# Linear attention and an MLP on one core: loads moved to ACT's queue, the reciprocal moved behind two decode steps, the drain reordered

## The chip, the cores and the metric

The kernel runs on one core of one Trainium2 chip. The metric is the device time of one execution in microseconds: 1163.93 us as the median of 3 runs before the change (1163.46 to 1164.61). Five engines work side by side, each through its own instructions in order: PE (matrix products; PEld is its weight load), DVE (vector), ACT (activations), POOL (GpSimd) and SP (which here only issues transfers). An engine that comes to an instruction whose input is not there stops until it is. A transfer (DMA) is issued by an engine into that engine's queue and then moved by 16 DMA engines that all queues share.

## What is computed

```python
def _attn_ref(q, k, v, w_phi):                     # q, k, v: 8 batches x 8 heads x 576 x 64
    def phi(x):
        proj = np.einsum('bhsd,df->bhsf', x, w_phi)                  # w_phi: 64 x 128
        proj = proj - np.max(np.abs(proj), axis=-1, keepdims=True)
        return np.concatenate([np.exp(proj), np.exp(-proj)], axis=-1)
    q_p, k_p = (phi(q), phi(k))
    kv = np.einsum('bhsf,bhsd->bhfd', k_p, v)
    z = np.sum(k_p, axis=2)
    num = np.einsum('bhsf,bhfd->bhsd', q_p, kv)
    den = np.einsum('bhsf,bhf->bhs', q_p, z)[..., None] + 1e-06
    return (num / den).astype(np.float32)

def _moe_ref(x, w_in, w_out):                      # x: 4608 x 512, d_ff = 2048
    h = x @ w_in
    g = h - np.tanh(h)
    return (g @ w_out).astype(np.float32)
```

The attention output, with heads side by side, is the input x of the MLP. The MLP's weights come as float64 and are brought to float32 on the chip.

## The kernel before

**Attention.** The 64 batch-head pairs are worked off as 32 units of two heads. Unit i needs `qk` (both projections' inputs, 576 KB, `load`, L192) and `v` (320 KB, `load_v`, L198). A software pipeline works on five units at once: `period(i)` (L454) names them `a` = unit i, `c` = i-1, `p` = i-2, `r` = i-3 and `q` = i-4. `ramp` starts the pipeline with units 0 to 2, periods 3 to 31 follow, `drain` empties it. Everything from `ramp` to `drain` stands in one block in which every engine executes in the order of the code, so a line moved in `period` moves on its engine and nowhere else.

In a period, on PE: `project(a)` into the PSUM banks `pj`, `pa` and `pt`; the denominators of `r` (`pu`, L341); the sums of `p`'s keys (L299); the turning of `p`'s kv matrix (L316) and of `c`'s projections (`ptt`, L247); `kv(c)` (`pc`, L278); the numerators of `p` (`po`, L327). On DVE: `centre` (the absolute maximum `m`, L235, and the subtraction, L236, which gives `t`) for the three parts; the copy of `kv`; then the reciprocal of the denominators, L365; then three functions of the weight decode. On ACT: the copy `dd` of the denominators (L355), `kst` (L305), the decode's first step (`dec_0`, L171), the exponentials of queries and keys, and the copy `d` of the numerators (L351). On POOL: `kadd` (four sums of the exponentials of `c`'s keys, L288 to L291), then the multiplication of numerators by reciprocals (`den_mul`, L379).

**The path of a quotient.** PE leaves the denominators of `r` in four PSUM rows. `denom_copy` brings them to `dd`, a transfer spreads them over 128 partitions (`dn`, L360), DVE takes the reciprocal (`rn`, L365), a transfer stores it in DRAM (`rr`, L370); in the next period two transfers read it back, repeated over 64 partitions each (`rb`, L375), POOL multiplies, and the product is stored in `xs` (L382), from where the MLP reads x (`xl`, L112). There is one `dd` buffer, and two of `d`, so the copy `d` of unit p waits for the multiplication of unit q.

**The weight decode.** One 128 x 512 tile of `w_in` or `w_out` (512 KB as float64, `raw`, two buffers) is decoded in each period: `dec_0` on ACT into the second half of the bank `pt`, after `centre` has read the first; `dec_1` (two instructions, L175 and L176), `dec_2` (L179) and `dec_3` (L183, into the tile `wi` or `wo`) on DVE. The next period's `project(a)` writes the same bank `pt`, so its last part waits for `dec_3`. In periods 4 to 17 ACT and POOL also split one decoded tile into a high and a low part (L90, L96).

**Transfers.** All of them are issued by SP in the order of the code, but for the projection weights `wph`, which ACT issues at the start. SP too executes in order: an issue that waits holds up those behind it.

**The MLP.** x is worked off in nine groups of 512 tokens, each through 16 tiles of the 2048 hidden units: 12 matmuls into `ph` (L599), the activation on ACT and DVE, the split into `gh` and `gl` (L627, L628), 12 matmuls into `po` (L642 to L645). Each x tile is split into high and low parts by `x_split` (ACT's cast, L117; DVE's subtraction, L118). The first group's four tiles are loaded in period 30 and split in the drain.

## Time and profile before

| | |
|---|---|
| median of 3 runs | 1163.93 us (1163.46 to 1164.61) |
| profiled execution: its time / its span | 1164.22 us / 1162.3 us |
| PE, PEld busy | 1109.3 us (95%), 866.5 us (75%) |
| DVE, ACT, POOL busy | 837.1 us (72%), 771.1 us (66%), 439.2 us (38%) |
| steady attention periods (first `pj` of period 4 to that of 31) | 39.85 to 344.20 us |
| MLP with PE busy throughout | from about 388 us to the end |
| mean granted PE clock | 0.994 |

A row of the timeline reads: start, duration, engine, line, operation, output<-input with shapes, and in brackets how long the engine stood idle before it and which instruction ended that wait. "SPq" and "ACTq" are the issues of transfers by SP and ACT. In the chain of waits a DMA's row runs from its issue to its landing. A row of the groups by line gives the busy time, the mean of one instruction in ns, and the idle time ahead of the group with its releasers. A matmul's end is modelled, so the start of the next one is the better mark. Line numbers are those of the kernel before.

### The profile page before, as it was taken

To read this page: it belongs to the slowest core of one execution; us is meant where nothing else is said; L and a number is where in the kernel's file an instruction comes from. 1 tells how busy PE (TensorE), PEld (TensorE's weight loads), DVE (VectorE), ACT (ScalarE), POOL (GpSimd) and SP (SyncE) were. 2 spreads that over 40 slices of the span, in tenths; PEclk is the share of its full clock that TensorE was granted. 3 is DMA by queue.
4 is the path that set the end of the run, shared out by engine and by line. 5 is a ranking of instruction groups with operands and counts; after the bars stand their busy time and mean duration, and the time that the engine had idled before them with its cause. 6 is when DMAs were issued, how large, how long until landed. Compare 5 with 4: busy or idle time off the path is not lost.

```text
span 1162.3 us, 18558 instructions
## 1 busy us (share of the span) xinstructions
PE 1109.3 (95%) x6956; PEld 866.5 (75%) x6956; DVE 837.1 (72%) x1166; ACT 771.1 (66%) x1394; POOL 439.2 (38%) x349
## 2 busy tenths in 40 slices
PE   7989898888989999999999999999999999999997
PEld 5656565555665788888888888888888888888886
DVE  5777778777787976766766766766766766776664
ACT  4767676666666776666666666666666666666664
POOL 4676767555554554232222222222222222222222
PEclk9999999999999999999999999999999999999999
DMA  5456566565655001101001001001001001000000
GB/s 185 137 169 201 167 188 185 179 187 168 195 160 164 16 1 37 48 31 37 37 1 37 37 1 37 37 1 37 36 1 39 34 1 41 33 1 7 31 1 37
DMA packets 51018, 85.45 MB, mean 74 GB/s; under 512 B 13296, under 2 KB 24688, under 8 KB 50928
## 3 DMA queue, kind: packets, MB, share of 16 engines
q1 hardware_dynamic: 50768, 84.20, 23.4%
q8 instruction: 55, 0.90, 0.3%
q14 instruction: 35, 0.29, 0.1%
q10 hardware_dynamic: 160, 0.07, 0.0%
HBM read 65.08 MB, written 19.02 MB: 72 GB/s over the span
## 4 chain that ended last, share of the span: by engine, by line
PE 72%; DMA 14%; DVE 10%; ACT 2%; issue 1%; SPq 1%; POOL 0%; POOLq 0%; ACTq 0%; DVEq 0%
PE ph L599 33%; DMA dn<-dd 12%; PE po L642 11%; PE po L645 11%; PE po L643 11%; PE pu L341 2%; DVE pt L179 2%; DVE pt L176 2%; DVE t L236 1%; DVE m L235 1%; DVE pt L175 1%; PE pt L219 1%; DVE wi L183 1%; DVE wo L183 1%; PE pc L316 1%
## 5 line engine op out<-in xcount | busy, mean ns | idle before, releaser
L628 POOL TENSOR_TENSOR gl<-s,gh 128x512 fp32r<-128x512 f32 x144 | 185.9, 1292 | 556.2 <-ACT gh L627 547.7
L606 ACT ACTIVATE y<-ph 128x512 f32<-128x512 f32 x144 | 86.2, 599 | 252.2 <-PE ph L599 252.2
L615 DVE SCALAR_TENSOR_TENSOR s<-s,y 128x512 f32<-128x512 f32 x144 | 102.3, 710 | 186.5 <-ACT s L608 185.4
L599 PE MATMUL ph<-xh,whi 128*128 128x512 f32 x576 | 224.3, 389 | 0.4 <-DVE s L621 0.4
L642 PE MATMUL po<-who,gh 128*128 128x512 f32 x572 | 222.8, 389 | 1.8 <-ACT gh L627 1.8
L599 PE MATMUL ph<-xl,whi 128*128 128x512 f32 x576 | 224.1, 389 | 0.0
L599 PE MATMUL ph<-xh,wli 128*128 128x512 f32 x576 | 224.1, 389 | 0.0
L643 PE MATMUL po<-wlo,gh 128*128 128x512 f32 x572 | 222.6, 389 | 0.0
L645 PE MATMUL po<-who,gl 128*128 128x512 f32 x572 | 152.9, 389 | 0.0
L621 DVE COPY_PREDICATED s<-mk,th 128x512 f32<-128x512 uint32 x128 | 122.5, 957 | 13.4 <-DVE th L620 0.5
L642 PEld LDWEIGHTS po<-who,gh 128*128 128x128 f32 x572 | 107.4, 188 | 25.0 <-ACT gh L627 2.7
L599 PEld LDWEIGHTS ph<-xh,whi 128*128 128x128 f32 x576 | 108.0, 187 | 23.6 <-DVE s L621 0.8
L599 PEld LDWEIGHTS ph<-xl,whi 128*128 128x128 f32 x576 | 108.2, 188 | 22.5
L599 PEld LDWEIGHTS ph<-xh,wli 128*128 128x128 f32 x576 | 108.1, 188 | 22.4
L645 PEld LDWEIGHTS po<-who,gl 128*128 128x128 f32 x572 | 107.4, 188 | 22.4
L643 PEld LDWEIGHTS po<-wlo,gh 128*128 128x128 f32 x572 | 107.3, 188 | 22.2
L608 ACT ACTIVATE s<-y,bias_t 128x512 f32<-128x512 f32 x144 | 104.4, 725 | 0.5 <-POOL gl L628 0.5
L614 ACT ACTIVATE mk<-y,bias_t 128x512 f32<-128x512 f32 x144 | 103.4, 718 | 1.4 <-DVE s L621 1.4
L618 DVE SCALAR_TENSOR_TENSOR s<-s,ph 128x512 f32<-128x512 f32 x144 | 98.8, 686 | 5.2
L617 DVE SCALAR_TENSOR_TENSOR s<-s,s 128x512 f32<-128x512 f32 x128 | 89.0, 695 | 16.2 <-ACT s L610 3.5
L272 ACT ACTIVATE kp<-t 128x1024 f32<-128x1024 f32 (+1 forms) x128 | 90.5, 731 | 11.7 <-DVE t L236 10.5
L610 ACT ACTIVATE s<-y,bias_t 128x512 f32<-128x512 f32 x128 | 92.2, 720 | 0.9 <-POOL gl L628 0.9
(98 smaller groups left out, 1701.9 us busy)
## 6 DMA issues: line engine op xcount, KB each, us to landing
qk<-in_qkT SPq DMA_DIRECT2D x31, 576.0 KB, 4.2
v<-in_v SPq DMA_DIRECT2D x32, 320.0 KB, 5.3
rb<-rr SPq DMA_DIRECT2D x64, 144.0 KB, 4.8
xs<-rb SPq DMA_DIRECT2D x32, 288.0 KB, 2.2
out<-o SPq DMA_DIRECT2D x36, 256.0 KB, 2.0
rawi<-in_moe_w_in SPq DMA_DIRECT2D x16, 512.0 KB, 4.2
rawo<-in_moe_w_out SPq DMA_DIRECT2D x16, 512.0 KB, 4.6
xl<-xs SPq DMA_DIRECT2D x24, 256.0 KB, 4.2
```

What stands on the lines that cost most here:

```text
L272: nc.scalar.activation(u.kp[h, :, j, s, :], u.t[r][h, :, x, :], AF.Exp, scale=1.0 - 2.0 * s)
L599: nc.tensor.matmul(h, wt[:, c * P : (c + 1) * P], x[:, c, 0:N], start=(i == 0), stop=(i == 3 * NCT - 1))
L608: nc.scalar.activation(s1, y, AF.Square, bias=bias_t[:, 0:1])
L610: nc.scalar.activation(s2, y, AF.Square, bias=bias_t[:, 1:2])
L614: nc.scalar.activation(mk, y, AF.Relu, bias=bias_t[:, 2:3])
L615: nc.vector.scalar_tensor_tensor(s1, s1, PC1, y, ALU.add, ALU.mult)
L618: nc.vector.scalar_tensor_tensor(gs, gs, PA, h, ALU.mult, ALU.mult)
L621: nc.vector.copy_predicated(gs, mk.bitcast(U32), hh)
L628: pin(nc.gpsimd.tensor_tensor(gl, gs, f32(gh), ALU.subtract))
L642: nc.tensor.matmul(po[t], a, wo[f][0], start=(f == 0), stop=False)
L643: nc.tensor.matmul(po[t], a, wo[f][1], start=False, stop=False)
L645: nc.tensor.matmul(po[t], gl[:, t * P : (t + 1) * P], wo[f][0], start=False, stop=(f == NF - 1))
```

## The change

1. `wph` is laid out on the host with both copies and loaded by ACT in one transfer of 128 rows.
2. In every period, the weight load and the load of `qk` are issued by ACT, behind the (optional) weight cast and ahead of `dd`. The weights of a decode are thereby loaded one period ahead of their use, where it was two. The ramp loads one weight tile where it loaded two.
3. On SP, `v` is loaded behind `dn` where it was ahead.
4. On DVE, the reciprocal runs behind `dec_1` and `dec_2` and ahead of `dec_3`; `rr`'s store follows it.
5. Period 31 and the drain: the x tiles are split earlier (the first two in period 31, the others ahead of the second-last decode); the second half of the last unit's key exponentials moves behind `kst` into the drain; `kv_copy`, `num_copy` and the load of `dn` stand in other places.

**SP in a steady period.** `rb` opens the period; `dn` is the load of the denominators; `xs` is the store of the product. Before:

```order
L375 DMA rb_744<-rr_719 64x576 x2
L200 DMA v_747<-in_v 128x640
L196 DMA qk_773<-in_qkT 128x1152
L360 DMA dn_801<-dd_799 128x1x9
L370 DMA rr_850<-rn_848 128x9
L382 DMA xs_76<-rb_744 128x576
L164 DMA rawo_858<-in_moe_w_out 128x512
```

Now:

```order
L375 DMA rb_741<-rr_721 64x576 x2
L360 DMA dn_798<-dd_796 128x1x9
L200 DMA v_800<-in_v 128x640
L370 DMA rr_852<-rn_850 128x9
L382 DMA xs_76<-rb_741 128x576
```

`qk` and the weights are gone from SP, and `v` stands behind `dn`. **ACT in the same period**, from the last key exponentials to the decode's first step, now:

```order
L272 ACTIVATE kp_114<-t_1_697 128x2x4x128
L90 CAST whi_738<-wi_724 128x512
L159 DMA rawi_779<-in_moe_w_in 128x4x128
L196 DMA qk_781<-in_qkT 128x1152
L355 ACTIVATE dd_796<-pu,bias_t 128x288
L305 COPY kst_802<-pu 128x128
L171 ACTIVATE pt_765<-rawo_648 128x512
```

The two DMA rows are what was added there; before, `dd` followed the cast.

**DVE from the last subtraction of a period to the next period's first maximum.** Before:

```order
L236 TENSOR_TENSOR t_1_829<-pa_761,m_1_751 128x1024
L365 RECIPROCAL rn_848<-dn_801 128x9
L175 TENSOR_SCALAR pt_770<-pt_770 128x512
L176 TENSOR_SCALAR pt_770<-pt_770 128x512
L179 SCALAR_TENSOR_TENSOR pt_770<-rawo_596,pt_770 128x512
L183 SCALAR_TENSOR_TENSOR wo_856<-rawo_596,pt_770 128x512
L235 TENSOR_REDUCE m_0_881<-pj_883 128x2x4
```

Now:

```order
L236 TENSOR_TENSOR t_1_828<-pa_756,m_1_746 128x1024
L175 TENSOR_SCALAR pt_765<-pt_765 128x512
L176 TENSOR_SCALAR pt_765<-pt_765 128x512
L179 SCALAR_TENSOR_TENSOR pt_765<-rawo_648,pt_765 128x512
L365 RECIPROCAL rn_850<-dn_798 128x9
L183 SCALAR_TENSOR_TENSOR wo_855<-rawo_648,pt_765 128x512
L235 TENSOR_REDUCE m_0_876<-pj_878 128x2x4
```

The reciprocal went three instructions down. PE's and POOL's orders are the same in both kernels from the first instruction to the last.

The diff, cut to its core:

```diff
-        nc.scalar.dma_start(wph[0:D, :], w_phi)
-        nc.scalar.dma_start(wph[D:P, :], w_phi)
+        nc.scalar.dma_start(wph, w_phi2)
...
         def ramp():
-            dec.extend(dec_load(n) for n in range(2))
+            dec.append(dec_load(0))
...
         def period(i):
             if q:
                 den_spread(q)
-            if i > 3:
-                load_v(a)
             project(a, "jat" if i > 3 else "ajt")
-            if i + 2 < NU:
-                load(units[i + 2])
             centre(a, "jt")
             kadd(c)
             if q:
                 den_mul(q)
             if low:
                 low()
+            dec.append(dec_load(i - 2, nc.scalar))
+            if i + 2 < NU:
+                load(units[i + 2], nc.scalar)
             pu = bank()
...
                 denom_copy(r)
                 den_recip_load(r)
+            if i > 3:
+                load_v(a)
             ksum_copy(p)
...
             k_exp(a, 1, (0,))
+            dec_1(w)
+            dec_2(w)
             if r:
                 den_recip(r)
                 den_store(r)
             if q:
                 x_store(q)
-            dec_1(w)
-            dec_2(w)
             dec_3(w)
-            dec.append(dec_load(i - 1))
+            if i == NU - 1:
+                for j in range(NCT // 2):
+                    x_split(xt[0], j)
             if i == NU - 2:
                 xt[0] = x_tiles(0)
                 for j in range(NCT):
                     x_load(0, xt[0], j)
             num(p)
             num_copy(p)
-            k_exp(a, 1, (1,))
+            if i < NU - 1:
+                k_exp(a, 1, (1,))
...
         def drain():
             q, r, p, c = units[-4:]
-            kadd(c)
             den_spread(q)
-            den_mul(q)
             pu = bank()
             denom(r, pu)
             ksum(p, pu)
             denom_copy(r)
             den_recip_load(r)
             ksum_copy(p)
+            k_exp(c, 1, (1,))
+            kadd(c)
+            den_mul(q)
+            dec.append(dec_load(NU - 2, nc.scalar))
...
+            kv_copy(c)
             num(p)
             x_store(q)
             den_spread(r)
             den_mul(r)
-            dec.append(dec_load(NU - 1))
-            for j in range(NCT // 2):
+            dec.append(dec_load(NU - 1, nc.scalar))
+            for j in range(NCT // 2, NCT):
                 x_split(xt[0], j)
-            kv_copy(c)
...
             denom_copy(p)
+            den_recip_load(p)
             x_store(r)
-            den_recip_load(p)
             num(c)
-            for j in range(NCT // 2, NCT):
-                x_split(xt[0], j)
...
-        "w_phi": inputs["w_phi"],
+        "w_phi": _np.concatenate([inputs["w_phi"], inputs["w_phi"]]),
```

## The prediction

> **What bounds the kernel now.** I first cut the span into stages with the view of windows; shown are the steady attention periods and the MLP (core time, busy time of PE, PEld, DVE, ACT and POOL with instruction counts, granted clock, DMA share, GB/s).

> ```profile
> 39.85:344.20 304.35, 268.34 (x2945) 180.96 (x2943) 234.62 (x325) 205.90 (x393) 193.90 (x149) 0.99 0.60 180
> ...
> 388.00:1162.30 774.30, 767.96 (x3385) 634.57 (x3383) 542.41 (x763) 511.22 (x901) 206.59 (x159) 1.00 0.07 24
> ```

> The MLP, 774.3 us, keeps PE busy throughout and the diff leaves it alone: I count it as fixed. What can move is the ramp ahead of the first row, the steady periods, and the drain between the two. The groups by line, for the steady stretch alone, say how many periods there are and who waits (busy, mean ns, then idle before and its releaser):

> ```profile
> L236 DVE TENSOR_TENSOR t<-pj,m 128x1024 f32<-128x1024 f32 x27 | 33.1, 1224 | 0.9
> L365 DVE RECIPROCAL rn<-dn 128x9 f32<-128x9 f32 x27 | 5.8, 215 | 59.4 <-DMA dn<-dd 59.4
> L219 PE MATMUL pt<-wph,qk 64*128 64x128 f32 x108 | 13.3, 323 | 28.3 <-DVE wi L183 20.7 <-DVE wo L183 7.6
> ```

> So 27 periods of 304.35/27 = 11.27 us. DVE stands 59.4/27 = 2.20 us in each at the reciprocal, waiting for `dn`, and PE stands 28.3/27 = 1.05 us because the weight decode behind that reciprocal still holds the `pt` bank. The chain of waits (start, us, piece) shows that this is a closed loop, one turn per period:

> ```profile
> 201.44 5.00 DMA dn<-dd
> 206.46 0.22 DVE rn L365
> 206.68 0.60 DVE pt L175
> ...
> 208.77 0.70 DVE wo L183
> 209.51 0.49 PE pt L219 x4
> 210.00 1.11 PE pu L341 x16
> ...
> 212.44 5.65 DMA dn<-dd
> ```

> `dn` lands, reciprocal, four decode steps (2.8 us), `pt` projection, denominators, their copy, next `dn`. Nothing in it needs the decode to follow the reciprocal; only DVE's order says so.

> **What a period costs without that wait.** The trace has one: in the first steady period `dn` of the period before had come early. The timeline:

> ```profile
> 39.85 1.16 PE L219 MATMUL pj<-wph,qk 64*128 64x128 f32 x16
> 41.06 1.23 DVE L235 TENSOR_REDUCE m<-pj 128x8 f32<-128x1024 f32 x1 [0.46 <-PE pj L219]
> 41.54 0.61 ACT L90 CAST whi<-wi 128x512 fp32r<-128x512 f32 x1
> 43.57 0.50 ACT L355 ACTIVATE dd<-pu,bias_t 128x288 f32<-128x288 f32 x1 [1.43 <-issue]
> 44.16 0.59 SPq L360 DMA_DIRECT2D dn<-dd  x1
> 47.92 1.42 POOL L379 TENSOR_TENSOR rb<-d,rb 128x576 f32<-128x576 f32 x1 [0.83 <-DMA rb<-rr]
> 48.82 0.21 DVE L365 RECIPROCAL rn<-dn 128x9 f32<-128x9 f32 x1 [1.69 <-DMA dn<-dd]
> 49.27 1.16 PE L219 MATMUL pj<-wph,qk 64*128 64x128 f32 x16
> 49.48 0.62 ACT L351 COPY d<-po 128x576 f32<-128x576 f32 x1
> ```

> From `pj` to `pj`: 49.27 - 39.85 = 9.42 us, with the full work of a period, PE waiting for no decode. DVE had 0.46 us to spare there, ACT 1.43 us (idle before `dd`). The floor is therefore 9.42 us, and the most the steady stretch can give is 27 x (11.27 - 9.42) = 50 us. That includes the two periods in which PE's idling cost its clock too, as these windows show (granted clock third from the end: 1.00, then 0.56 just after PE stood idle):

> ```profile
> 84.00:86.00 2.00, 0.17 (x4) 0.00 (x0) 1.93 (x4) 0.00 (x0) 1.92 (x2) 1.00 0.42 150
> 86.00:88.00 2.00, 1.88 (x16) 1.00 (x20) 1.97 (x3) 0.62 (x1) 1.86 (x2) 0.56 0.28 67
> ```

> **Term 1, the reciprocal behind two decode steps.** Three DVE instructions now run ahead of it: 206.68 to 208.77, 2.09 us, against a mean wait of 2.20. In the free period DVE came to the reciprocal at 48.82 - 1.69 = 47.13; it would now come at 49.22, and with its 0.46 us to spare may be held until about 49.7 before PE feels it. `dd` ended at 44.07, so `dn` may take 5.6 us to land. What it takes, from the same chain (first and last of 26 in the stretch, the shortest, the longest, and one with the queues empty):

> ```profile
> 44.16 4.63 DMA dn<-dd
> ...
> 224.92 4.24 DMA dn<-dd
> ...
> 234.92 6.56 DMA dn<-dd
> ...
> 349.62 5.58 DMA dn<-dd
> ...
> 371.34 1.89 DMA dn<-dd
> ```

> Eight of the 26 exceed 5.6 us; the excess averaged over all is 0.17 us. If `dn` lands no sooner than now, the period is 9.42 + 0.17 = 9.59. If every one took 6.56 it would be 10.38; if none exceeded 5.6, 9.42. Term 2 argues for sooner, but the engines, pressed into shorter periods, argue for later, so I take 9.59: 27 x 1.68 = **45.4 us gained**, bounds 24 and 50.

> **Term 2, the queues.** SP drops `qk` and the weights, and `v` goes behind `dn`, so `dn` is issued when `dd` is there (0.1 us sooner in the free period) with only `rb` ahead of it in its queue, where 512 KB of weights, 320 of `v` and 576 of `qk` stood before. I give this no gain of its own beyond the 9.59. The issues cost ACT time in order, ahead of `dd`. By line (ns: min/median/max), for `rb` with the time to landing, and last `rr`'s row of the page (KB, us to landing):

> ```profile
> L196 SPq DMA_DIRECT2D qk<-in_qkT x33: 327/376/977, 0.7 to 326.2; - x33
> L375 SPq DMA_DIRECT2D rb<-rr x64: 444/572/2047, 41.1 to 496.2; - x64
> DMA to landing us min/median/max: 3.0/4.8/6.5
> ...
> L395 ACTq DMA_DIRECT2D wph<-in_w_phi x1: 611/611/611, 1.3 to 1.3; - x1
> ...
> rr<-rn SPq DMA_DIRECT2D x32, 4.5 KB, 1.4
> ```

> Two issues at 0.38 (SP's median) to 0.61 (ACT's own, under load) are 0.8 to 1.2 us; ACT's gap before `dd` is 1.43 in a period with a weight cast (the first 14) and longer by that cast's 0.61 in the others. So: nothing, hidden by that gap; without it, up to 1.2 us a period. Queued behind on ACT are `dd`, the `kst` copy and the decode's first step, for which SP, PE and DVE wait. `qk` waits for the last projection, which ends before `dd`'s denominators begin on PE, so it adds no wait. Loads have ample time: weights are wanted one period later, `qk` nearly two.

> `rb` is the other short path: the reciprocal, 2.1 us later, delays `rr` and so `rb`. For the period quoted, the reciprocal before would run at 49.22 - 9.42 = 39.80, `rr` be issued at 40.0 and land 1.4 later (last row above), and `rb`'s second half be issued 0.57 on, near 42.0. It lands between 45.0 and 48.5; POOL is free for the multiply from 47.92 - 0.83 = 47.09, so that ends between 48.5 and 49.9, and ACT's `d` copy at 49.48 needs it. Zero to 0.45 us; I take zero, since `rb` no longer queues behind weights, and keep 0.45 x 27 = 12 us for the range.

> [...]

> **Term 3, the start.** PE waited for the second half of `wph`:

> ```profile
> 4.06 0.60 PE L219 MATMUL pj<-wph,qk 64*128 64x128 f32 x2
> 1.32 6.12 DMA wph<-in_w_phi
> 7.49 1.66 PE L219 MATMUL pj<-wph,qk 64*128 64x128 f32 x13 [2.83 <-DMA wph<-in_w_phi]
> ```

> One load of all 128 rows, issued at 0.74, lands between 4.0 (as the first half) and 7.4 (if it is the rows, not the later issue, that took so long). Everything in the ramp follows the first projection. Gain 0 to 3.4; **I take 1.5 us**, somewhat under the middle.

> **Term 4, the drain.** PE's and POOL's orders are unchanged; ACT's moves. The stalls, and a pair of casts that it moves:

> ```profile
> 356.04 0.64 ACT L351 COPY d<-po 128x576 f32<-128x576 f32 x1 [2.10 <-POOL rb L379]
> 358.24 0.33 PE L308 MATMUL pu<-ident,kst 128*128 128x128 f32 x1 [1.98 <-ACT kst L305]
> 361.18 1.18 ACT L117 CAST xh<-xl 128x512 fp32r<-128x512 f32 x2
> 373.33 0.50 ACT L355 ACTIVATE dd<-pu,bias_t 128x288 f32<-128x288 f32 x1 [1.18 <-DMA dn<-dd]
> ```

> The `kst` copy stood behind ACT's 2.10 us wait, and PE idled 1.98 us for it. `rb` will be issued about 1 us sooner and one pair of x casts (1.18 us) now fills that wait, so PE's stall shrinks to a few tenths; but `k_exp`'s second half moves behind `kst`, and the last `kadd` (four POOL sums) with it, which caps the gain. **2 us**, from -1 (the casts simply add 1.2 on ACT) to 4 (all of PE's stall and the slow clock after it).

> **Sum.** 45.4 + 1.5 + 2 = 48.9 off the profiled execution's 1164.22 us (span 1162.3 and 1.9 around it): 1115.3; the median shown is 0.3 lower, so **1115.0 us**. Its own range: 50 + 3.4 + 4 = 57.4 gives 1106.5; periods of 10.0 (34.3), no gain at the start, 1 lost in the drain give 1130.6.

> **Rivals.** (A) *The new queue slows the small transfers.* Weights and `qk`, 1.09 MB, now move beside `rb` and `dn` rather than in a set order; `wph`'s 32 KB on ACT's queue took 6.12 us beside SP's loads, which speaks for it; that `dn` has nearly nothing ahead of it in its own queue speaks against. With `dn` at 6.56 every time: 10.38 us, 24 + 3.5 gained, 1136.4.

> (B) *ACT's issues stretch past its gap.* SP's `rb` issues reached 2.05 us. At 1.24 each (two make 2.48), the gap is overrun by 1.05 in 14 periods and 0.44 in 13, together 20.4: gain 50 - 20.4 + 3.5 = 33.1, 1131. Against it: SP's `qk` median is 0.38.

> (C) *The same place, slower than before.* ACT's room is 14 x 1.43 + 13 x 2.04 = 46.5 us over 54 issues; the gain to be eaten is 53.5. From (46.5 + 53.5)/54 = 1.85 us an issue the kernel is slower; at `rb`'s worst, 2.05, by 10.7: 1174.6. Only if ACT is stopped at every issue.

> (D) *It doesn't do what it says:* `dn` slips by the whole 2.2 us that was covered, and the loop closes as before: 3.5 off at most, 1160 to 1164. Nothing in the rows makes it slip so far.

> **Chances.** Forecast 0.68, A 0.16, B 0.09, C 0.04, D 0.03. Range 1107 to 1139: the forecast's own, widened to take in A and B. This kernel's runs differ by 0.1%, so 0.2% (2.3 us) is what can be told from no change. Faster 0.94, within 0.02, slower 0.04.

> **What would show it.** DVE's idle before the reciprocal should fall from 59.4 us to under 10, PE's before `pt` from 28.3 to under 8, `pj` to `pj` to 9.4 to 9.8, with no clock of 0.56 in the periods. If the reciprocal still waits over 1 us a period, A holds; if ACT's DMA issues exceed 0.7 us and PE waits for `kst`, B. First full `pj` before 6.5 us confirms term 3. I am wrong if the period stays above 10.2.

## The result and the profile after

The changed kernel takes 1122.24 us as the median of 4 runs (1118.34 to 1125.27), beside 1164.05 (1163.46 to 1164.61) for the kernel before: a ratio of 0.9639, 95% interval 0.9605 to 0.9673. It is 7.2 us above the predicted 1115.0. The profiled execution is the fastest of the four, 1118.34 us with a span of 1116.6. The changed kernel's runs differ by 0.6%, where those of before differed by 0.1%.

The view of windows, cut at the first `pj` of period 4, at that of period 31 and near the start of the MLP (core time, busy time of PE, PEld, DVE, ACT, POOL, granted clock, DMA share, GB/s):

```profile
0.00:36.36 36.36, 30.37 (x317) 21.45 (x317) 25.09 (x32) 21.44 (x40) 17.44 (x25) 1.00 0.49 165
36.36:299.23 262.87, 256.39 (x2946) 178.19 (x2944) 234.29 (x325) 205.42 (x393) 194.14 (x149) 1.00 0.72 208
...
343.00:1116.60 773.60, 766.57 (x3378) 633.40 (x3377) 540.92 (x761) 510.52 (x899) 206.24 (x159) 1.00 0.07 24
```

The first `pj` of period 4 starts at 36.36 (39.85 before): 3.5 us gained in the ramp. The 27 periods take 262.87 us (304.35 before): 41.5 gained, a mean period of 9.74. From there to the end it is 1116.6 - 299.23 = 817.4 (818.1 before): 0.7 gained. Together 45.7, the difference of the spans. The clock is 1.00 throughout: no slow stretch is left in the periods.

The groups by line of the periods (busy, mean ns, idle before and its releaser):

```profile
L365 DVE RECIPROCAL rn<-dn 128x9 f32<-128x9 f32 x28 | 5.8, 206 | 0.2 <-DMA dn<-dd 0.2
L219 PE MATMUL pt<-wph,qk 64*128 64x128 f32 x108 | 10.5, 272 | 0.0
...
L219 PE MATMUL pa<-wph,qk 64*128 64x128 f32 x432 | 29.4, 276 | 6.3 <-ACT d L351 6.3
L351 ACT COPY d<-po 128x576 f32<-128x576 f32 x27 | 17.0, 631 | 8.3 <-POOL rb L379 7.1 <-PE pj L219 0.9 <-PE po L327 0.2
```

DVE's 59.4 us before the reciprocal are 0.2, PE's 28.3 before `pt` are nothing: the loop through `dn` is gone, with nothing left of it. A new wait of PE stands in its place, 6.3 us before `pa`, which waits for ACT's copy `d`, which waits for POOL's multiplication (7.1). In the periods before the change PE had no wait at `pa`:

```profile
L219 PE MATMUL pa<-wph,qk 64*128 64x128 f32 x432 | 28.8, 273 | 0.0
```

The waits of the changed kernel in its periods (us in total, times, longest) say what POOL waited for, and one more thing, on ACT:

```profile
ACT dd L355 <- PE pu L299: 43.9, 27, 1.9
...
POOL rb L379 <- DMA rb<-rr: 7.4, 4, 2.5
POOL rb L379 <- issue: 7.1, 6, 2.4
```

`dd` waits 1.6 us a period for PE, so the two issues ahead of it on ACT cost nothing. POOL waits for `rb`; where the view says "issue", it names no releaser. In one of the stalled periods the timeline shows the new chain whole:

```profile
269.80 1.40 POOL L379 TENSOR_TENSOR rb<-d,rb 128x576 f32<-128x576 f32 x1 [2.70 <-PE po L327]
271.23 0.64 ACT L351 COPY d<-po 128x576 f32<-128x576 f32 x1 [1.62 <-POOL rb L379]
271.92 1.16 PE L219 MATMUL pa<-wph,qk 64*128 64x128 f32 x16 [1.46 <-ACT d L351]
```

`PE po` is named as POOL's releaser, but that matmul had long ended; it was `rb`, whose second half was issued at 262.0. In the chain of waits the longest transfers of the periods are now of `rb`, but the chain's row for this one, 5.10 us from 262.00, is too short: such a row can break off where the waiting engine ended its previous instruction (POOL at 267.1), so it is not always the time to landing. The rows of the issue, for the pair at 126.3 and for this one, give the landings:

```profile
L375 SPq DMA_DIRECT2D rb<-rr x2: 465/531/597, 126.3 to 126.8; - x2
...
DMA to landing us min/median/max: 6.4/7.1/7.7
```

```profile
L375 SPq DMA_DIRECT2D rb<-rr x2: 466/532/599, 261.5 to 262.0; - x2
...
DMA to landing us min/median/max: 5.7/6.7/7.7
```

The second half took 7.7 us and landed at 269.7, where POOL goes on.

18 of the 27 intervals from `pj` to `pj` are at the floor of 9.42 us; the other nine are 9.49 to 11.12 and hold the excess, 262.87 - 27 x 9.42 = 8.5 us; in seven of the nine PE waits at `pa`.

### The profile page after: what moved, and what is told of

The parts are those of the page before. It is cut to its first block, busy times and chain, and to the rows that moved or that the text cites. A ratio compares the mean times of both kernels' runs of the same rounds, so it can differ in the third digit from the quotient of the medians.

```text
span 1116.6 us, 18536 instructions
## 1 busy us (share of the span) xinstructions
PE 1094.2 (98%) x6956; PEld 861.5 (77%) x6956; DVE 835.9 (75%) x1166; ACT 770.6 (69%) x1394; POOL 439.6 (39%) x349
## 4 chain that ended last, share of the span: by engine, by line
PE 83%; DVE 6%; DMA 5%; issue 2%; POOL 1%; ACT 1%; SPq 0%; POOLq 0%; DVEq 0%; ACTq 0%
PE ph L605 34%; PE po L648 11%; PE po L651 11%; PE po L649 11%; PE pc L278 4%; DMA rb<-rr 3%; PE po L327 3%; DVE m L235 2%; PE pj L219 2%; DVE t L236 2%; PE pu L341 2%; PE pa L219 2%; PE ptt L247 1%; DMA rr<-rn 1%; POOL rb L379 1%
```

## The experiments

Each kernel was timed in several rounds beside the kernel before on the same chip; ratios are to that, with 95% intervals. "The floor" is 9.42 us from `pj` to `pj`.

**1. The reciprocal alone.** The kernel before, with the reciprocal and what follows it put behind two decode steps; no transfer moved to another queue.

```diff
             k_exp(a, 1, (0,))
+            dec_1(w)
+            dec_2(w)
             if r:
...
                 x_store(q)
-            dec_1(w)
-            dec_2(w)
             dec_3(w)
```

> The kernel before with one edit: the reciprocal, the store of rr and the store of x stand behind the decode's second and third step (one two-instruction step, one single). All transfers stay on SP in the old order. Theory 1 (the order on DVE closed the loop): DVE's wait at the reciprocal falls from 2.2 us to under 0.5 us a period, PE no longer waits for the decode, the period goes from 11.27 to 9.6-10.2 us, the time to 1119-1135 us. Theory 2 (dn lands late because of what stands ahead of it in SP's queue, and will simply be late by as much again): the wait at the reciprocal stays above 1.5 us, the period above 10.8, the time above 1151 us.

1124.0 us (1119.79 to 1128.48), ratio 0.965 [0.9614, 0.9685]; mean period 9.75, 14 of 27 at the floor. This one edit gives nearly all of the change's gain, as theory 1 expected. The groups by line, 36 to 300 us:

```profile
L365 DVE RECIPROCAL rn<-dn 128x9 f32<-128x9 f32 x27 | 5.8, 214 | 11.5 <-DMA dn<-dd 11.1
...
L379 POOL TENSOR_TENSOR rb<-d,rb 128x576 f32<-128x576 f32 x26 | 36.8, 1416 | 22.8 <-DMA rb<-rr 22.5
```

The wait for `dn` falls from 59.4 us to 11.1, not to 0.2: three decode steps' time covers most of `dn`, not all. The forecast's allowance for `dn` of 0.17 us a period (4.6 us in all) was meant for a `dn` like this one. PE's largest wait in the periods is again at `pa` (4.5 us), through `d` and `rb` as in the whole change.

**2. The transfers alone.** The other half: weights and `qk` through ACT's queue, `v` behind `dn`, one weight tile fewer ahead (in the ramp too); the reciprocal stays ahead of the decode.

```diff
-            if i > 3:
-                load_v(a)
             project(a, "jat" if i > 3 else "ajt")
-            if i + 2 < NU:
-                load(units[i + 2])
...
+            dec.append(dec_load(i - 2, nc.scalar))
+            if i + 2 < NU:
+                load(units[i + 2], nc.scalar)
...
                 den_recip_load(r)
+            if i > 3:
+                load_v(a)
...
-            dec.append(dec_load(i - 1))
```

> The kernel before with the transfers alone changed: weights and qk issued by ACT ahead of dd, v behind dn on SP. The reciprocal stays ahead of the decode, wph in two loads, drain as before. In the chain of waits a period is dn's landing time plus about 6.0 us. Theory 1 (dn shares the DMA engines with whatever moves, whoever issued it): dn takes 4.5-5.2 us, the period is 10.4-11.1 us, the time 1141-1160 us. Theory 2 (its own queue ahead of dn was what made it late): dn takes 3.5 us or less, the period reaches 9.4-9.5 us and the time is under 1120 us.

1123.54 us (1118.26 to 1129.26), ratio 0.9661 [0.9611, 0.9711]; mean period 9.63, 16 at the floor. Neither expectation held (10.4 to 11.1 us a period, or 9.4 to 9.5). This edit too gives nearly the whole gain by itself, far more than the forecast's term 2 gave it (nothing). So the two halves are not added: either opens the loop through `dn`, and the second then finds little left to gain. The reciprocal's row:

```profile
L365 DVE RECIPROCAL rn<-dn 128x9 f32<-128x9 f32 x27 | 5.8, 213 | 12.6 <-DMA dn<-dd 12.5
```

Why does the reciprocal wait so much less, without having been moved? SP's timeline (issues: start, duration) in a period of the kernel before:

```profile
142.60 0.33 SPq L164 DMA_DIRECT2D rawo<-in_moe_w_out  x1
142.99 1.10 SPq L375 DMA_DIRECT2D rb<-rr  x2
144.19 0.53 SPq L200 DMA_DIRECT2D v<-in_v  x1
144.82 0.98 SPq L196 DMA_DIRECT2D qk<-in_qkT  x1
145.89 0.59 SPq L360 DMA_DIRECT2D dn<-dd  x1
```

and in this experiment, where the weights and `qk` are issued by ACT at 143.09 and 144.40:

```profile
141.87 1.10 SPq L375 DMA_DIRECT2D rb<-rr  x2
146.27 0.58 SPq L360 DMA_DIRECT2D dn<-dd  x1
```

In the kernel before, the load of the weights waits on SP for the decode's last step, whose buffer it overwrites. SP's waits over the whole span (us in total, times, longest) are 1.9 us for each load:

```profile
SPq L159 <- DVE wi L183: 29.5, 15, 2.4
SPq L164 <- DVE wo L183: 26.0, 14, 2.0
```

All behind it is held, and then 512 KB of weights, 288 of `rb`, 320 of `v` and 576 of `qk` go out within 3.3 us just ahead of `dn`. The decode is itself behind the reciprocal that waits for `dn`. There was thus a second loop in the kernel, through SP: late `dn`, late decode, late weights, a packed burst, late `dn`. The prediction saw only the first. Either edit opens both: with the reciprocal alone moved (1), SP waits 0.3 us in all for the decode's last step in the periods.

**3. The projection weights alone.**

```diff
-        nc.scalar.dma_start(wph[0:D, :], w_phi)
-        nc.scalar.dma_start(wph[D:P, :], w_phi)
+        nc.scalar.dma_start(wph, w_phi2)
```

> The kernel before with wph in one load of 128 rows and nothing else. Theory 1 (everything in the ramp follows the first projection): first full projection at 4.3 us instead of 7.5, the start of the steady periods 3.5 us sooner, time 3.5 us less, 1160.5 us. Theory 2 (later transfers of the ramp set its end): under 1 us is left, above 1163 us.

1161.47 us (1158.23 to 1163.63, 10 runs), ratio 0.9968 [0.995, 0.9986]. The timeline of PE:

```profile
4.09 2.01 PE L219 MATMUL pj<-wph,qk 64*128 64x128 f32 x16
```

The first full `pj` starts at 4.09 us and that of period 4 at 36.61, 3.2 us sooner than before. So it was the second transfer that came late, not the 128 rows. How late it comes differs from profile to profile: over the six kernels with two transfers the full projection goes on at 4.98 to 7.57 us. The first `pj` of period 4 follows at 37.37 to 40.70 us there, but not in step with it, and at 35.94 to 36.72 in the six kernels with one transfer. So this part is worth 0.7 to 4.8 us by the profiles, and three of the six kernels with two transfers also load one weight tile fewer in the ramp; by the times of this experiment it is 1.6 to 5.8 us (the interval of the ratio), with theory 1's 3.5 inside.

**4. One spare copy of `d`.** The changed kernel with three `d` buffers, so that a late `rb` no longer holds the copy; one spare weight tile was given up for the room.

```diff
-    wpool = ctx.enter_context(tc.tile_pool(name="wpool", bufs=2 * NF + 2))
+    wpool = ctx.enter_context(tc.tile_pool(name="wpool", bufs=2 * NF + 1))
...
-            u.d = tail.tile([P, S], F32, tag="d", name=f"d{u.i}", bufs=2)
+            u.d = tail.tile([P, S], F32, tag="d", name=f"d{u.i}", bufs=3)
```

> The changed kernel with three buffers for d instead of two (and one spare weight tile fewer, to make room), so that the copy of the numerators does not wait for the POOL multiplication of the unit two earlier. In the changed kernel's profile the steady periods take 9.74 us in the mean against 9.42 at best; the 8.5 us above it lie in the few periods in which ACT waits for POOL and POOL for rb. Theory 1 (that one buffer is the whole path from rb to PE): every period 9.42-9.45 us, time 1109-1114 us, runs within 1 us of each other. Theory 2 (a late rb finds another way to PE: POOL's sums come late, or rb's own buffers): under 3 us gained, 1117 us or more.

1118.32 us (1117.63 to 1122.25), ratio 0.9607 [0.9584, 0.963]: the interval overlaps the change's, so nothing is separated, as theory 2 expected. The profiled run is the slowest of its four, with a mean period of 9.87. In it the wait at `pa` is gone, but a late `rb` finds another way. SP's timeline:

```profile
115.58 0.32 SPq L382 DMA_DIRECT2D xs<-rb  x1
115.95 3.97 SPq L375 DMA_DIRECT2D rb<-rr  x2
120.02 0.58 SPq L360 DMA_DIRECT2D dn<-dd  x1
```

`xs` waits on SP for the multiplication, `rb` of the next period is issued behind it and its two issues take 3.97 us, and `dn`, whose `dd` was there at 117.44, goes out 2.6 us late; the reciprocal waits again:

```profile
L365 DVE RECIPROCAL rn<-dn 128x9 f32<-128x9 f32 x28 | 6.0, 214 | 23.9 <-DMA dn<-dd 23.8
```

Taking away the wait for the buffer alone doesn't help: the late `rb` then reaches PE through SP and `dn`.

**5. The transfers alone, on SP.** Experiment 2 with the periods' weights and `qk` issued by SP at the same place of the code: the order without the second queue. (The drain's two weight loads stay on ACT, as in experiment 2.)

```diff
-            dec.append(dec_load(i - 2, nc.scalar))
+            dec.append(dec_load(i - 2))
             if i + 2 < NU:
-                load(units[i + 2], nc.scalar)
+                load(units[i + 2])
```

> The kernel of the run with the transfers alone changed (weights and qk issued ahead of dd's copy, v behind dn, reciprocal ahead of the decode), but in the steady periods weights and qk are issued by SP at that same place, so that dn stands behind them in one queue. That run took 9.63 us a period, 1123.5 us. Theory 1 (the second queue is what lets dn land sooner): dn lands in 5 us or more again, the period, landing time plus about 6.0 us, is 10.9-11.2 us, the time 1153-1162 us. Theory 2 (it was the order alone: weights one period later, v out of dn's way): period 9.6-9.9 us, time 1119-1129 us.

1121.78 us (1119.57 to 1123.47), ratio 0.9636 [0.9615, 0.9656], against 0.9661 [0.9611, 0.9711] with the queue. Theory 2 held: the queue gives nothing that can be measured (the two intervals overlap almost whole); the order alone is enough for the gain. The rows of `rb`'s issue and landing in this kernel, no worse than with two queues (a median of 3.1 us here, 3.3 in experiment 2):

```profile
L375 SPq DMA_DIRECT2D rb<-rr x64: 445/512/1631, 38.6 to 453.8; - x64
...
DMA to landing us min/median/max: 2.8/3.1/4.8
```

**6. The big loads behind `dn`.** The changed kernel with weights and `qk` issued by SP behind `dn` and `v`.

```diff
-            dec.append(dec_load(i - 2, nc.scalar))
-            if i + 2 < NU:
-                load(units[i + 2], nc.scalar)
...
                 load_v(a)
+            dec.append(dec_load(i - 2))
+            if i + 2 < NU:
+                load(units[i + 2])
```

> The changed kernel with weights and qk issued by SP, in the order dn, v, weights, qk: one queue, nothing large ahead of rb or dn, ACT issues nothing in the steady periods. Theory 1 (what counts is that nothing large is in flight when rb and dn are issued): rb lands in 4 us or less, ACT's waits for POOL disappear, the period is 9.42-9.55 us, time 1112-1118 us. Theory 2 (rr then stands behind 1.4 MB in SP's queue, and rb starts late): period 9.9 us or more, time above 1127 us.

1114.92 us (1110.83 to 1116.64), ratio 0.9573 [0.9547, 0.9599], just apart from the change's interval (0.9605 to 0.9673). `rb`'s median time to landing goes from 5.3 us to 3.1. The rows of the two issues, in the changed kernel for `rb`, and here for `rb` and `rr`:

```profile
L375 SPq DMA_DIRECT2D rb<-rr x64: 444/550/621, 37.9 to 449.8; - x64
...
DMA to landing us min/median/max: 2.9/5.3/7.7
```

```profile
L375 SPq DMA_DIRECT2D rb<-rr x64: 445/511/1857, 37.4 to 448.2; - x64
...
DMA to landing us min/median/max: 2.8/3.1/5.0
...
L370 SPq DMA_DIRECT2D rr<-rn x32: 320/326/377, 36.0 to 446.3; - x32
DMA to landing us min/median/max: 1.4/3.1/5.9
```

But `rr`, 4.5 KB, now goes out behind the big loads and lands in 3.1 us, at worst 5.9, where it took 1.4 before. `rb` can only be issued when `rr` is there, and `pa` still waits, with two periods of 10.9 and 11.6:

```profile
ACT d L351 <- POOL rb L379: 7.0, 7, 2.3
...
PE pa L219 <- ACT d L351: 5.3, 7, 2.0
```

The waits for POOL that theory 1 expected to disappear are 7.0 us, beside 7.1 in the change, and the mean period is 9.71, beside 9.74 and the expected 9.42 to 9.55. The two profiles differ by 2.2 us, only 0.6 of them in the periods. So the medians say that this kernel is about 7 us faster, but its profile doesn't show where: the change's profile is of its fastest run, this one of its second slowest.

**7. ACT's issues in the middle of its chain.** The changed kernel with the two issues behind the decode's first step, where ACT's instructions follow each other with hardly a gap.

```diff
-            dec.append(dec_load(i - 2, nc.scalar))
-            if i + 2 < NU:
-                load(units[i + 2], nc.scalar)
...
             dec_0(w, a.pt)
+            dec.append(dec_load(i - 2, nc.scalar))
+            if i + 2 < NU:
+                load(units[i + 2], nc.scalar)
```

> The changed kernel with ACT's two issues moved from the gap ahead of dd to behind the decode's first step, where ACT's instructions follow each other without a gap. It prices the issues where nothing covers them. Theory 1 (ACT's chain from dd to the copy of the numerators has no room, so the two issues, 0.33 and 0.39 us, add in full): period 10.1-10.3 us, time 1131-1139 us. Theory 2 (they are hidden there too, and a cleaner start for rb gains): period 9.4-9.75 us, 1115-1124 us.

1118.21 us (1116.97 to 1119.74), ratio 0.9609 [0.9587, 0.9631]. Only 8 periods are at the floor, the mean is 0.31 us above it, where the two issues last about 0.9 (0.39 and a median of 0.52): about a third of their time at most reaches PE, and the slowdown that theory 1 expected for this place did not come; theory 2 held. The time is that of the change within the noise. `rb` gains meanwhile: with the big loads some 7 us ahead of it, where the change has the weights 1 us ahead (145.74 and 146.74 in one period), its median is 3.2 us:

```profile
L375 SPq DMA_DIRECT2D rb<-rr x64: 445/552/1885, 38.3 to 449.3; - x64
...
DMA to landing us min/median/max: 2.9/3.2/6.3
```

So in these kernels `rb`'s landing goes by what was issued just ahead of it, on whichever queue: 5.3 us in the change; 3.1 and 3.2 with the loads moved away on SP (6) or on ACT (7); and 3.3 in experiment 2, where the loads are on ACT as in the change but the earlier reciprocal puts `rb` ahead of them (141.87, then 143.09).

**8. Both remedies.** Experiment 6 with the three `d` buffers of experiment 4 (the same two lines).

> The run with all loads on SP behind dn, and three buffers for d (one spare weight tile fewer). With three d alone the time was 1118.3 us, its periods still 9.87 us in the profile, because a late rb holds up SP and with it dn. Theory 1 (with rb and dn both early nothing is left above PE's own 9.42 us): period 9.42-9.47 us, time 1110-1114 us. Theory 2 (rr and rb late in SP's queue): no better than the run without the third buffer, 1118 us or more.

1111.81 us (1110.35 to 1116.32), ratio 0.9558 [0.953, 0.9585]: as theory 1 expected, and about 10 us under the change, whose interval begins at 0.9605. 24 of 27 periods are at the floor, none is above 9.86, the mean is 9.47. The window of its periods:

```profile
36.50:292.12 255.62, 255.07 (x2946) 176.93 (x2944) 233.31 (x325) 204.08 (x393) 194.09 (x149) 1.00 0.65 214
```

PE is busy for all but 0.6 us of 255.62, and the excess over the floor is 255.62 - 27 x 9.42 = 1.3 us: nearly all of what the periods can give is used. Against the change's profile this one gains 7.3 us in the periods. That takes both edits: the third buffer alone (4) and the order alone (6) left 9.87 and 9.71 us a period in their profiles.

**9 and 10. Which transfer made `dn` late.** The kernel before with one transfer moved each: in 9 only `v`, behind `dn`; in 10 only the load of the weights, to the next period's start, where its buffer is free by then (and, with that, one weight tile fewer in the ramp).

```diff
-            if i > 3:
-                load_v(a)
             project(a, "jat" if i > 3 else "ajt")
...
                 den_recip_load(r)
+            if i > 3:
+                load_v(a)
```

> The kernel before with one edit: the load of v stands behind dn on SP. In the kernel before, SP's weight issue waits for the decode's last step, and rb, v, qk and dn follow it within about 3.3 us: some 1.7 MB ahead of dn. Theory 1 (it is that wait of the weight issue that packs everything in front of dn): taking 0.32 MB out of the pack brings dn about 1 us sooner, the period goes from 11.27 to about 10.3 us, time 1132-1150 us. Theory 2 (v in front of dn was the whole of it): period 9.6-9.9 us, time 1119-1129 us.

```diff
             project(a, "jat" if i > 3 else "ajt")
+            dec.append(dec_load(i - 2))
             if i + 2 < NU:
...
             dec_3(w)
-            dec.append(dec_load(i - 1))
```

> The kernel before with one edit: the weight load is issued by SP in the next period, behind v and ahead of qk, where it has nothing to wait for; rb is then issued as soon as rr has landed. v and qk and now the weights stand ahead of dn in the same queue, and the reciprocal ahead of the decode. Theory 1 (the waiting weight issue was what packed the transfers): period 9.6-10.1 us, time 1119-1133 us. Theory 2 (bytes ahead of dn in its queue are what counts, and these are not fewer): period 10.9 us or more, time above 1153 us.

9 takes 1146.17 us (1145.39 to 1146.94), ratio 0.9833 [0.9816, 0.9851], mean period 10.57; 10 takes 1130.96 (1128.01 to 1132.06), ratio 0.9694 [0.9671, 0.9718], mean period 10.18. Both times are within what theory 1 expected. The reciprocal's row in the one and in the other:

```profile
L365 DVE RECIPROCAL rn<-dn 128x9 f32<-128x9 f32 x27 | 5.8, 215 | 41.2 <-DMA dn<-dd 41.2
```

```profile
L365 DVE RECIPROCAL rn<-dn 128x9 f32<-128x9 f32 x27 | 5.8, 215 | 27.7 <-DMA dn<-dd 27.7
```

The weight load's place alone is worth 33 us, `v`'s alone 18, against about 41 for all transfers (experiment 2). In 10 SP's waits of the weight load for the decode's last step are gone, in 9 they are still 48.9 us. That the place of that waiting load was the larger part of the lateness of `dn` is shown; the parts again do not add (18 + 33 is more than 41), since all are cut off at the same floor.

## Why the prediction was right, and where not

**Bound and floor.** Right. No period in any kernel went under 9.42 us, the one free period that the trace of before showed, and experiment 8 reaches 9.47 as a mean.

**Term 1 (45.4 us; 41.5 measured).** The mechanism was right: DVE's and PE's waits went as named, and the reciprocal alone does it (experiment 1). The size was made of two errors, so that it came out near is in part luck. The 4.6 us kept for a late `dn` (0.17 us a period) were not needed: DVE's wait there is 0.2 us in all 27 periods, since the transfers' order takes most of the lateness of `dn` away (2); I had given it no gain. Against it stands the step that failed, in term 2: "Zero to 0.45 us; I take zero, since `rb` no longer queues behind weights". `rb` no longer queues behind weights on SP, but weights from ACT, issued 1 us ahead of it, go with a landing as slow: its median is 5.3 us, not less than the 4.8 of before, and its longest 7.7, past the 6.5 that bounded the estimate. The 2.1 us by which the reciprocal was put back then had to come out of a path with little to spare, and most of the 8.5 us above the floor were lost there (6.3 us of waits at `pa`), within the 12 kept for the range. The path (`rr`, `rb`, POOL, `d`) was named; that PE meets it at `pa` was not.

**Term 2 (no gain of its own).** In the sum it holds, since the reciprocal alone already reaches most of the floor. As a statement on the transfers it was wrong: alone they are worth 41 us. I costed the issue of `dn` by the free period, in which SP waited for nothing, and so saw 0.1 us; in a stalled period SP's own wait for the decode (1.9 us a load) packs 1.7 MB into the 3.3 us ahead of `dn`. Had I read the waits of SP, the second loop would have been seen. ACT's issues cost nothing where the change puts them, as forecast (`dd` waits 1.6 us a period for PE).

**Term 3 (1.5 us; 3.5 in this profile, 3.2 in experiment 3).** Under-estimated: the bound "as the first half" was the right one for the landing. What it is worth differs with the profile of before that one compares with (experiment 3).

**Term 4 (2 us; 0.7 in this profile).** From the first `pj` of period 31 to the end, the five kernels with the new drain (the change, 4, 6, 7 and 8) take 816.2 to 817.4 us, 816.8 in the mean; the seven with the old one 816.5 to 820.4, 818.5 in the mean (818.1 before). The means differ by 1.7, near the 2 that was forecast, but one kernel with the old drain (10) is at 816.5, and no run changes the drain alone: the sign agrees, the size is not settled.

**Sum.** 41.5 + 3.5 + 0.7 = 45.7 against 48.9: 3.2 us less than forecast, and the profiled execution, at 1118.34, is 3.3 above the 1115.0 that was forecast for the median. The median of the four runs is 3.9 above that execution. Only the fastest was profiled, so where the others lost their 2 to 7 us isn't shown. `rb` is the one transfer on PE's path in its trace, and is the likely place; but experiment 8, with `rb` off that path, still spreads by 6 us, so the spread's cause stays open.

**Rivals.** A, "the new queue slows the small transfers", is half right: `rb` is slowed, by the loads' place in time and not by the queue (a median of 5.3 us in the change, 3.1 in 5 and 6, 3.2 in 7). `dn` costs nothing: DVE waits 0.2 us for it, so rival A's price, every `dn` at 6.56 and felt, did not come; when it landed can't be read where nothing waits for it. B and C fall: ACT's issues keep to 0.33 to 0.53 us in the change, and even in a place without a gap they cost less than they last (at most 0.31 us of about 0.9, experiment 7). D falls.

## What to carry to other kernels

Here a transfer's issue that waited on SP (1.9 us a load) held up everything behind it, and 1.7 MB then went out within 3.3 us; read the waits of the issuing engine in a stalled period, not in a free one, before a transfer order is costed at nothing. Two edits that open the same loop do not add: each alone was worth about 41 us here, and both together, with the start and the drain, 42, so ask of each whether the other leaves it anything. When a short transfer is on the path, place the large loads so that none is issued just ahead of it, and give its consumer a spare buffer. Here `rb` landed in a median of 4.8 us behind weights issued 0.4 us ahead of it on SP (the kernel before, at 142.60 and 142.99), in 5.3 behind weights issued 1 us ahead on ACT (the change), and in 3.1 to 3.3 with no load issued just ahead of it (2, 5, 6 and 7). By the medians of the times, the one gave 7 us here and the two together 10, and only the two together brought the periods to the floor.

## What the runs showed of the hardware

**The smallest transfer was not spared.** `rr`, 4.5 KB, lands 1.4 us after its issue in every period of the kernel before, and in 3.1 (median) to 5.9 behind the big loads on the same queue (experiment 6).

**The length of a stall alone didn't decide whether the clock dropped.** Before the change PE stood idle 1.95 us until 86.12, and the windows of 1 us show the granted clock (third from the end) at 0.50 to 0.67 in the next four:

```profile
86.00:87.00 1.00, 0.88 (x8) 0.61 (x12) 1.00 (x2) 0.62 (x1) 0.92 (x2) 0.63 0.03 12
87.00:88.00 1.00, 1.00 (x12) 0.39 (x8) 0.97 (x2) 0.00 (x0) 0.94 (x1) 0.50 0.52 123
88.00:89.00 1.00, 1.00 (x16) 0.39 (x8) 0.97 (x3) 0.00 (x0) 0.98 (x1) 0.50 1.04 368
89.00:90.00 1.00, 1.00 (x13) 0.75 (x6) 0.27 (x2) 0.56 (x3) 0.30 (x1) 0.67 1.11 269
```

That is 0.37 + 0.50 + 0.50 + 0.33 = 1.7 us more, nearly the stall again. In experiment 6 PE was idle 2.01 us until 88.07, and in the same execution as the rows above 2.19 us until 336.13; both times the clock stayed whole (1.00 in experiment 6's windows from 82 to 93 us, and here):

```profile
336.13 0.49 PE L219 MATMUL pt<-wph,qk 64*128 64x128 f32 x4 [2.19 <-DVE wi L183]
```

```profile
332.00:335.42 3.42, 1.95 (x32) 1.75 (x32) 2.23 (x5) 1.68 (x3) 1.58 (x2) 1.00 0.28 91
335.42:338.83 3.41, 2.39 (x32) 1.42 (x33) 3.35 (x4) 0.66 (x2) 3.25 (x3) 1.00 0.40 125
338.83:342.24 3.41, 3.41 (x33) 2.42 (x33) 3.11 (x4) 2.94 (x6) 0.84 (x2) 1.00 0.72 212
```

In experiment 3 a stall of 1.77 us, shorter than both, was followed by slow matmuls: the 16 into `pu` took 1.44 us, where they took 1.18 behind a stall of 1.68 us (until 60.74):

```profile
83.19 0.49 PE L219 MATMUL pt<-wph,qk 64*128 64x128 f32 x4 [1.77 <-DVE wi L183]
83.62 1.44 PE L341 MATMUL pu<-qe,ks 128*32 128x288 f32 x16
```
